# Second-stage products of a fused retention and MLP kernel cut in two, and the figures of its plan set anew

## The chip, the cores and the metric

The kernel runs on one core of a Trainium2 chip, in one launch. The metric is the device time of the launch in microseconds, the median of the runs. TensorE (PE in the profile) multiplies, VectorE (DVE) and ScalarE (ACT) work on what it leaves in PSUM, GpSimd (POOL) and SyncE (SP) issue the DMAs.

## The reference

The first part is retention, attention without a softmax: for each of 8 batches and 8 heads, over 576 positions and 64 dimensions. Its output, with the heads side by side, is the input of an MLP of 4608 tokens, 512 wide, with 2048 hidden units and the exact gelu.

```python
scores = scale * np.matmul(q, k.transpose(0, 1, 3, 2))
gamma = 1.0 - 2.0 ** (-5.0 - np.arange(H))
Dmat = np.where(rel >= 0, gamma[:, None, None] ** rel[None, :, :], 0.0)   # rel = i - j
x = np.matmul(scores * Dmat, v)              # to (4608, 512)
h = x @ w_in                                 # (4608, 2048)
g = 0.5 * h * (1.0 + erf(h / sqrt(2)))
out = g @ w_out                              # (4608, 512), float32
```

## The kernel before

**Work.** The 4608 tokens are nine blocks of 512 (t = 0 to 8), four units of 128 tokens each. For a unit, q and k are turned (by TensorE for the first ten units, by a transposing DMA after that), TensorE makes the scores (tile sc), VectorE multiplies them by the mask (ret), TensorE adds what lies within the chunk and what comes from the running state (o_ps, u_ps), and VectorE or ScalarE writes the result as a part of xT. The values scaled by the decay (vh) are made by ScalarE for the units in VH_ACT, in eight small instructions, and by VectorE for the others, in one.

**First MLP stage.** x times w_in. Blocks 0 and 1 take it plainly. From block 2 on the hidden units come in four parts, kp = 0 to 3, and each part is done in one of two ways. Either plainly, as 16 products of 512 columns with their gelus (`laid`, "p3" in LAYOUTS). Or as a set of seven products of half size in place of eight, by Strassen's scheme (`unit`, `add_chain`): 28 products of 256 columns on sums of x (xs) and of w_in (wi_sum), in three PSUM banks Y, Z and X. VectorE and ScalarE work between the products: the product 4 may only be added to its bank when q has been formed, 5 when the bank Y has been copied (m3), 6 when dif has been formed, 7 when the gelu c21 has read the bank Z (BEHIND). In LAYOUTS "0" is the set of part 0 by itself, "12" two sets woven, "p3" the plain part 3.

**Second MLP stage.** g times w_out, also by seven half-size products from block 1 on (FAST). The tokens of a block are cut into two halves, the columns of w_out as well; sums of g (tile s, `g_sum`) and of w_out (w_sum) are made by VectorE. A product p of SECOND = "1267534" contracts over four parts kp of two rows of 128, for each of r = 0 and 1: eight products of 256 columns. `fast` (line 1144) issues these eight in one piece. The sums of g stand in two tiles, one for kp 0 and 1 and one for kp 2 and 3, and a piece waits for both. VectorE and ScalarE bring the banks together (`add_second`), and SP stores the rows.

**What sets the order.** A planner in the kernel itself (class Plan, and the loop at the end) gives each step a duration, what it depends on and a due time, and runs engine by engine through time as it issues the instructions. What it reckons has no effect on the chip but through the order in which each engine's instructions stand. The figures: HOT is the time up to which TensorE is reckoned at half clock (`slow`), FETCH and BUSY_FETCH what the refill of a page of TensorE's instructions is reckoned to take (`paged`, PAGE = 127.8 products), 0.1 us for a change of array mode (`pe_time`, `run_woven`), GAP_A and GAP_B the least distance between two attention steps made of many small products, APART the groups whose scores are not woven with the step before, LOOK how many pieces ahead the loop may pick, HOLD, BEFORE, LEAD, SPREAD and EASE due times, SLACK how far a later step may be preferred by its due time. ORDER is the order of the loads on POOL's queue; of these, at most eight are on their way at once (`room_to_fly`). While the loads of the opening arrive, `warm` fills TensorE's gaps with products of zeros.

In a piece of the second stage:

```python
for kp in range(4):
    for kk in range(2):
        product(c[:, at, :], lhsT=left(t, p, kp)[:, kk, r * 128:r * 128 + 128],
                         rhs=right(p, kp)[:, kk, :], ...)
```

Of the kernel before, what the change touches and what calls it, by code (L numbers as in the profile page):

```python
# [107 lines left out]
def kernel(  # L108
# [23 lines left out]
    N_BLK = n_tok // TOK  # L132
# [28 lines left out]
    def slot_of(i):  # L161
# [3 lines left out]
    n = v_order.index(pair_of[1, 1][0])  # L165
# [5 lines left out]
    N_VH = 5  # L171
    N_RET = 3
    N_Q = 4
    VH_ACT = [5, 6, 7, 8, 9, 10, 16, 17, 19, 20, 23, 25, 27, 29, 30, 31, 32, 33, 34, 35, 36, 37]
    HOT = 9.2
    N_WARM = 8
    SLACK = 0.05
    CUTS = (0, 128, 256, 384, 512)
    AHEAD = 5
    VH_DUE = 14.0  # L180
    PARTS = 4
    FAST = 1
    FETCH = 3.5
    BUSY_FETCH = 6.2
    GAP_A = 1.6
    GAP_B = 1.6
    APART = [6, 7]
    BEFORE = 3.7
    UNIT_FROM = 2
    LOOK = 6  # L190
    HOLD = 5.0
    LAYOUTS = {2: ['0', '12', 'p3'], 3: ['0', '12', 'p3'], 4: ['01', '2', 'p3'], 5: ['01', '2', 'p3'], 6: ['23', '0', 'p1'], 7: ['0', '12', 'p3'], 8: ['0', '12', 'p3']}
    LEAD = 8
    SPREAD = 6.7
    EASE = 9
    ORDER = ("q1 q2 pos k2 q3 k3 v3 wi0 k1 wi4 v2 v1 wi5 wi1 wi2 wi3 wi6 v4 k5 wi7 q5 q4 wo0 k4 v5 wo4 wo1 wo5 wo2 "
             "q9 wo6 q6 wo7 v10 v7 q8 k7 v6 wo3 k6 v9 q7 k10 k9 v8 k8 q10").split()
    K_ORDER = [0, 1, 8, 9, 2, 3, 10, 11, 4, 5, 12, 13, 6, 7, 14, 15]
    PRODUCTS = "3251467"
    SECOND = "1267534"  # L200
    LAYOUT = {t: ["p0", "p1", "p2", "p3"] for t in range(2, N_BLK)}
    for t in range(UNIT_FROM, N_BLK):
# [15 lines left out]
    P = Plan()  # L218
    P.later = {}
    T = P.T  # L220
# [24 lines left out]
    banks = [f"b{n}" for n in range(8)]  # L245
# [57 lines left out]
    stream = []  # L303
    for t in range(N_BLK):
        if t < 2:
            cuts = CUTS if t == 0 else (0, 256, 512)
            for lo, hi in zip(cuts, cuts[1:]):
                stream.append([("1", t, m, 2, lo, hi) for m in K_ORDER[::2]])
        else:
            stream.append([one for block in LAYOUT[t] for one in laid(t, block)])  # L310
        if t < FAST:
            stream.append([("2", t, ts, m, m + 2) for m in range(0, N_DF, 2) for ts in range(2)])
            stream.append([("2", t, ts, m, m + 4) for ts in range(2, 4) for m in range(0, N_DF, 4)])
        else:
            stream.append([("2", t, p, r, n) for n, p in enumerate(SECOND) for r in range(2)])

    def piece_time(one):
        if one[0] == "u":
            return 4 * 0.1092
        if one[0] == "1":  # L320
            return one[3] * N_DM * ((one[5] - one[4]) / 2400 + 0.0025)
        return 8 * 0.1092 if isinstance(one[2], str) else (one[4] - one[3]) * 0.2158

    W0 = 14.0
    W = {}
# [27 lines left out]
    pos = const.tile([128, 1, NCI], FP32, name="pos")  # L353
# [518 lines left out]
    land = {}  # L872
# [268 lines left out]
    def rows_at_once(t):  # L1141
        return [(0, 1)] if t < N_BLK - 1 else [(0,), (1,)]

    def fast(one):
        _, t, p, r, _ = one
        rs = next(x for x in rows_at_once(t) if r in x)
        alone = p in "12"
        c = chain_of(("2", t, rs), [128, 1 if alone else len(rs), HALF], f"A{r}" if alone else BANK2[p])
        at = 0 if alone else r - rs[0]
        for kp in range(4):  # L1150
            for kk in range(2):
                product(c[:, at, :], lhsT=left(t, p, kp)[:, kk, r * 128:r * 128 + 128],
                                 rhs=right(p, kp)[:, kk, :], start=(p in OPENS and at + kp + kk == 0),
                                 stop=(kp == 3 and kk == 1), skip_group_check=True)
        if p == SECOND[-1] and r == 1:
            for two in range(2):
                g_ring[two].give(T["pe"] + 0.3)
                s_ring[two].give(T["pe"] + 0.3)
# [153 lines left out]
    for run in stream:  # L1312
        for one in run:
# [16 lines left out]
                    add_chain(("u", t, kp), 2, {q_: [f"mlp{('u', t, kp, q_)}"] for q_ in PRODUCTS},  # L1330
                              {q_: W["u", t, kp, q_] for q_ in PRODUCTS})
            elif isinstance(one[2], str):
                _, t, p, r, n = one
                rs = next(x for x in rows_at_once(t) if r in x)
                key = f"c{('2', t, rs)}"
                deps = []
                if p in G_SUM:
                    deps += [f"gs{t},{two}.{G_SUM[p]}" for two in range(2)]
                else:
                    deps += gelus_of(t, range(4), int(p != "1"))  # L1340
                deps += [f"ws{kp}.{W_SUM[p]}" for kp in range(4)] if p in W_SUM else []
                deps += [f"land wo{kp + 4 * (p != '1')}" for kp in range(4)] if p in "123" else []
                deps += [key + BEHIND2[p] + (str(r) if p == "2" else "")] if p in BEHIND2 else []
                add(nm, "pe", piece_time(one), deps, lambda one=one: fast(one), W[one], DRAIN,
                    banks=int(p == "1" or p in OPENS and r == rs[0]))
                if p == SECOND[-1] and r == rs[-1]:
                    at_ = {q_: {x: W["2", t, q_, x, SECOND.index(q_)] for x in rs} for q_ in SECOND}
                    add_second(("2", t, rs), len(rs), {q_: [f"mlp{('2', t, q_, x, SECOND.index(q_))}" for x in rs] for q_ in SECOND},
                               {q_: max(at_[q_].values()) for q_ in SECOND})
# [90 lines left out]
    in_macro = {nm for m in macros for nm in m[1]}  # L1440

    mode = ["full"]
    stretch_end = [0.0]

    def slow():
# [18 lines left out]
    def run_woven(names, start):  # L1464

        T["pe"] = start
        T["pe"] = T["now"] = start + weave(names) + (0.1 if mode[0] != "quad" else 0.0)
# [59 lines left out]
    def begun(one):  # L1527

        if one[0] == "u":
            return one[3] in "321" or BANK_OF[one[3]] in chain.get(one[:3], ())  # L1530
        if one[0] == "2" and isinstance(one[2], str):
            rs = next(x for x in rows_at_once(one[1]) if one[3] in x)
            return one[2] in "12" or (one[2] in OPENS and one[3] == rs[0]) or BANK2[one[2]] in chain.get(("2", one[1], rs), ())
        return True

# [43 lines left out]
    while True:  # L1579
# [72 lines left out]
```

## Time and profile before

| | us |
|---|---|
| median of 3 runs | 284.89 |
| lowest, highest | 284.52, 285.73 |
| the profiled execution | 285.15 |
| its span, first to last instruction | 283.2 |
| TensorE busy | 274.2 |
| VectorE busy | 224.5 |
| ScalarE busy | 182.7 |
| GpSimd busy | 110.3 |

The time of the profiled execution is longer than its span by what lies around the instructions. A row of the order in time gives the start, the time to the end of the last of the merged instructions, engine, line, operation, what is written from what, the shape, the count, and in brackets the idle time before with what ended it. Nearly all products carry line 229, a helper; they are told apart by the tiles: hT, yT, zT and xT_ belong to the first stage, oT to the second, sc, o_ps, u_ps and qk_ps to attention, warm to the fillers.

### The profile page before, as it was taken

To read this page: it belongs to the slowest core of one execution; us is meant where nothing else is said; L and a number is where in the kernel's file an instruction comes from. 1 tells how busy PE (TensorE), PEld (TensorE's weight loads), DVE (VectorE), ACT (ScalarE), POOL (GpSimd) and SP (SyncE) were. 2 spreads that over 40 slices of the span, in tenths; PEclk is the share of its full clock that TensorE was granted. 3 is DMA by queue.
4 is the path that set the end of the run, shared out by engine and by line. 5 is a ranking of instruction groups with operands and counts; after the bars stand their busy time and mean duration, and the time that the engine had idled before them with its cause. 6 is when DMAs were issued, how large, how long until landed. Compare 5 with 4: busy or idle time off the path is not lost.

```text
span 283.2 us, 8896 instructions
## 1 busy us (share of the span) xinstructions
PE 274.2 (97%) x3707; PEld 219.8 (78%) x3721; DVE 224.5 (79%) x430; ACT 182.7 (65%) x458; POOL 110.3 (39%) x139
## 2 busy tenths in 40 slices
PE   7999999999999999999999999999999999999993
PEld 2579848678888688868886888687868886888782
DVE  5760392689999997999799998986997788769832
ACT  7678805987318934795299329943898489727740
POOL 8966779809944059701426701905000000000000
PEclk9999999999999999999999999999999999999999
DMA  9999999999999999999999995999700040012013
GB/s 146 165 187 178 193 176 163 167 185 161 145 129 179 196 103 145 148 241 108 140 185 88 130 152 169 117 137 135 192 2 2 11 144 0 5 62 89 0 39 111
DMA packets 152071, 35.57 MB, mean 126 GB/s; under 512 B 141024, under 2 KB 147680, under 8 KB 152032
## 3 DMA queue, kind: packets, MB, share of 16 engines
q0 software_dynamic: 115792, 17.97, 96.2%
q1 hardware_dynamic: 35200, 16.78, 33.5%
q8 instruction: 29, 0.48, 0.8%
q10 hardware_dynamic: 1040, 0.26, 0.4%
q14 instruction: 10, 0.08, 0.1%
HBM read 36.70 MB, written 9.44 MB: 163 GB/s over the span
## 4 chain that ended last, share of the span: by engine, by line
PE 78%; DMA 11%; POOL 6%; issue 2%; ACT 1%; DVE 1%; POOLq 0%; ACTq 0%
PE oT L229 37%; PE hT L229 11%; PE zT L229 9%; DMA w_in<-in_moe_w_in_dram 6%; PE yT L229 6%; PE o_ps L229 4%; POOL qk_ld L517 3%; DMA w_out<-in_moe_w_out_dram 3%; PE sc L229 3%; PE u_ps L229 2%; DMA qk_ld<-in_k_dram 2%; POOL v_ld L517 1%; ACT g L1209 1%; PE qk_ps L233 1%; DVE t L568 0%
## 5 line engine op out<-in xcount | busy, mean ns | idle before, releaser
L229 PEld LDWEIGHTS <-w_in 128*128 128x128 bf16 x664 | 54.2, 98 | 14.8 <-issue 0.3
L229 PEld LDWEIGHTS <-g 128*128 128x128 bf16 x576 | 54.9, 98 | 12.5
L229 PE MATMUL hT<-xT,w_in 128*128 128x128 bf16 (+2 forms) x488 | 56.1, 267 | 0.4
L229 PEld LDWEIGHTS <-wi_sum 128*128 128x128 bf16 x420 | 40.9, 98 | 7.2 <-issue 0.9
L1099 ACT ACTIVATE g<-hT 128x512 bf16<-128x512 f32 (+1 forms) x76 | 37.9, 510 | 13.3 <-PE hT L229 11.5
L229 PE MATMUL oT<-w_out,g 128*128 128x256 bf16 (+1 forms) x315 | 44.0, 293 | 0.2 <-issue 0.2
L824 ACT ACTIVATE vh<-v_ld,dv 128x64 bf16<-128x64 bf16 x160 | 44.0, 344 | 0.0
L517 POOL DMA_DIRECT2D qk_ld<-in_q_dram x31 | 28.2, 909 | 39.7 <-DMA qkT<-qk_ld 29.9
L229 PEld LDWEIGHTS <-s 128*128 128x128 bf16 x384 | 36.9, 98 | 5.7 <-issue 1.0
L517 POOL DMA_DIRECT2D v_ld<-in_v_dram x31 | 28.3, 915 | 17.3 <-ACT vh L824 13.2
L229 PE MATMUL oT<-w_sum,s 128*128 128x256 bf16 x256 | 31.5, 273 | 0.7 <-issue 0.7
L1240 ACT COPY o_sb<-oT 128x512 f32<-128x512 f32 (+1 forms) x27 | 14.5, 539 | 26.9 <-PE oT L229 16.7
L229 PE MATMUL oT<-w_sum,g 128*128 128x256 bf16 x256 | 30.8, 273 | 0.0
L517 POOL DMA_DIRECT2D qk_ld<-in_k_dram x31 | 28.3, 914 | 1.5 <-DMA w_in<-in_moe_w_in_dram 0.6
L1209 ACT ACTIVATE g<-zT 128x512 bf16<-128x512 f32 x42 | 24.5, 619 | 0.4
L652 DVE TENSOR_TENSOR ret<-sc,msk 128x512 bf16<-128x512 f32 x36 | 23.0, 680 | 0.9 <-PE sc L229 0.9
L1244 DVE TENSOR_TENSOR o_sb<-o_sb,oT 128x512 f32<-128x512 f32 (+1 forms) x27 | 16.7, 623 | 8.3 <-PE oT L229 4.0
L570 ACT COPY q<-yT 128x512 f32<-128x512 f32 x17 | 9.9, 590 | 18.3 <-PE yT L229 18.3
L855 DVE TENSOR_TENSOR xT<-o_ps,dqT 128x512 bf16<-128x512 f32 x26 | 16.7, 680 | 3.0 <-PE o_ps L229 3.0
L568 DVE COPY qkT<-qk_ps 128x512 bf16<-128x512 bf16 x16 | 6.2, 418 | 15.4 <-PE qk_ps L233 15.4
L1218 DVE TENSOR_TENSOR zT<-q,zT 128x512 f32<-128x512 f32 x21 | 14.5, 692 | 1.6 <-PE zT L229 1.4
L829 ACT CAST u_sb<-u_ps 128x512 bf16<-128x512 f32 x15 | 8.8, 584 | 10.7 <-PE u_ps L229 7.1
(165 smaller groups left out, 457.7 us busy)
## 6 DMA issues: line engine op xcount, KB each, us to landing
out_dram<-o_sb SPq DMA_DIRECT2D x30, 256.0 KB, 4.1
qk_ld<-in_q_dram POOLq DMA_DIRECT2D x31, 128.0 KB, 6.5
qk_ld<-in_k_dram POOLq DMA_DIRECT2D x31, 128.0 KB, 6.3
v_ld<-in_v_dram POOLq DMA_DIRECT2D x31, 128.0 KB, 6.6
w_in<-in_moe_w_in_dram POOLq DMA_DIRECT2D x8, 256.0 KB, 8.3
w_out<-in_moe_w_out_dram POOLq DMA_DIRECT2D x8, 256.0 KB, 8.6
out_dram<-o_sb SPq DMA_DIRECT2D x12, 128.0 KB, 2.5
v_ld<-in_v_dram POOLq DMA_DIRECT2D x8, 64.0 KB, 5.7
```

The lines of the kernel that those rows point to most:

```text
L229: return nc.tensor.matmul(*args, **more)
L517: nc.gpsimd.dma_start(dst, src[2 * bp + j, :, ci * C:ci * C + C, :].rearrange("h s d -> s h d"))
L570: nc.scalar.copy(dst, src)
L652: nc.vector.tensor_tensor(r, t, by, op=ALU.mult)
L824: nc.scalar.activation(vh[:, h], loaded[i][1][:, h], AF.Copy, scale=dv[:, h, ci:ci + 1])
L829: ins = (nc.vector.tensor_copy if engine == "dve" else nc.scalar.copy)(u_sb[t if bp >= FINE else ci % 2], u_bank[1])
L855: nc.vector.tensor_tensor(dst, o, dqT[:, :, ci * C:ci * C + C], op=ALU.mult)
L1099: nc.scalar.activation(g_of(t, m0)[:, m0 % 2:m0 % 2 + n, m0 // 8, lo:hi], hT, AF.Gelu)
L1209: nc.scalar.activation(target(key, what), chain[key][n][1], AF.Gelu)
L1218: nc.vector.tensor_tensor(to, chain[key]["q"], z, op=ALU.add)
L1240: nc.scalar.copy(target(key, what), chain[key][n][1])
L1244: nc.vector.tensor_tensor(to, to, chain[key][n][1], op=ALU.add)
```

## The change

A piece of the second stage becomes two, part 0 for kp 0 and 1 and part 1 for kp 2 and 3. Each waits only for the sums of g, the gelus and the weights that it reads. The pieces of one product stay in their order. The figures of the plan, the parts of the first stage that are done as sets of seven (LAYOUTS: block 7 has four sets and no plain part), the units whose vh ScalarE makes, and the order of the loads are set anew; the change of mode is reckoned at 0.13 us (CHANGE), and loads that land early get 0.3 us of margin in the plan.

```diff
-    VH_ACT = [5, 6, 7, 8, 9, 10, 16, 17, 19, 20, 23, 25, 27, 29, 30, 31, 32, 33, 34, 35, 36, 37]
-    HOT = 9.2
+    VH_ACT = [5, 8, 12, 14, 15, 17, 19, 20, 26, 28, 30, 31, 32, 35, 37]
+    HOT = 10.1
-    SLACK = 0.05
+    SLACK = 0.3
-    FETCH = 3.5
+    FETCH = 4.0
-    GAP_A = 1.6
-    GAP_B = 1.6
-    APART = [6, 7]
-    BEFORE = 3.7
+    GAP_A = 4.2
+    GAP_B = 1.5
+    APART = [3, 6, 7]
+    BEFORE = 0.4
-    LOOK = 6
-    HOLD = 5.0
-    LAYOUTS = {2: ['0', '12', 'p3'], 3: ['0', '12', 'p3'], 4: ['01', '2', 'p3'], 5: ['01', '2', 'p3'], 6: ['23', '0', 'p1'], 7: ['0', '12', 'p3'], 8: ['0', '12', 'p3']}
+    LOOK = 16
+    HOLD = 4.6
+    LAYOUTS = {2: ['0', '12', 'p3'], 3: ['01', '2', 'p3'], 4: ['2', '30', 'p1'], 5: ['01', '2', 'p3'], 6: ['10', '2', 'p3'], 7: ['01', '23'], 8: ['3', '20', 'p1']}
-    SPREAD = 6.7
-    EASE = 9
-    ORDER = ("q1 q2 pos k2 q3 k3 v3 wi0 k1 wi4 v2 v1 wi5 wi1 wi2 wi3 wi6 v4 k5 wi7 q5 q4 wo0 k4 v5 wo4 wo1 wo5 wo2 "
-             "q9 wo6 q6 wo7 v10 v7 q8 k7 v6 wo3 k6 v9 q7 k10 k9 v8 k8 q10").split()
+    SPREAD = 7.1
+    EASE = 6.5
+    ORDER = ("q3 q2 k3 q1 pos v2 k2 wi0 k1 wi4 v3 v1 wi1 wi3 wi5 v4 wi2 wi6 k4 wi7 q4 wo0 q5 k5 v5 wo4 wo1 q9 q8 "
+             "wo5 v7 wo6 k7 wo7 v10 wo2 q6 v6 k6 wo3 q7 k10 q10 k8 k9 v9 v8").split()
-    PRODUCTS = "3251467"
+    PRODUCTS = "3251647"
...
-            stream.append([("2", t, p, r, n) for n, p in enumerate(SECOND) for r in range(2)])
+            stream.append([("2", t, p, r, n, part) for n, p in enumerate(SECOND) for r in range(2) for part in range(2)])
...
-        return 8 * 0.1092 if isinstance(one[2], str) else (one[4] - one[3]) * 0.2158
+        return 4 * 0.1092 if isinstance(one[2], str) else (one[4] - one[3]) * 0.2158
...
-        for kp in range(4):
+        for kp in (2 * part, 2 * part + 1):
...
-        if p == SECOND[-1] and r == 1:
+        second_left[t] -= 1
+        if not second_left[t]:
...
+                kps = (2 * part, 2 * part + 1)
                 if p in G_SUM:
-                    deps += [f"gs{t},{two}.{G_SUM[p]}" for two in range(2)]
+                    deps += [f"gs{t},{part}.{G_SUM[p]}"]
                 else:
-                    deps += gelus_of(t, range(4), int(p != "1"))
+                    deps += gelus_of(t, kps, int(p != "1"))
...
+    CHANGE = 0.13
...
-        return d + (0.1 if op.mode != mode[0] else 0.0)
+        return d + (CHANGE if op.mode != mode[0] else 0.0)
...
-            pad = MARGIN if op.name[0] == "v" and at > 40.0 else 0.0
+            pad = MARGIN if op.name[0] == "v" and at > 40.0 else 0.3 if flying[-1].end < 10.0 else 0.0
```

More of the change, by code (lines that the diff above doesn't have):

```diff
@@ L1142, in rows_at_once @@
         return [(0, 1)] if t < N_BLK - 1 else [(0,), (1,)]
+    second_left = dict.fromkeys(range(N_BLK), 28)
     def fast(one):
-        _, t, p, r, _ = one
+        _, t, p, r, _, part = one
         rs = next(x for x in rows_at_once(t) if r in x)
@@ L1332 @@
             elif isinstance(one[2], str):
-                _, t, p, r, n = one
+                _, t, p, r, n, part = one
+                kps = (2 * part, 2 * part + 1)
                 rs = next(x for x in rows_at_once(t) if r in x)
@@ L1337 @@
                 if p in G_SUM:
-                    deps += [f"gs{t},{two}.{G_SUM[p]}" for two in range(2)]
+                    deps += [f"gs{t},{part}.{G_SUM[p]}"]
                 else:
-                    deps += gelus_of(t, range(4), int(p != "1"))
-                deps += [f"ws{kp}.{W_SUM[p]}" for kp in range(4)] if p in W_SUM else []
-                deps += [f"land wo{kp + 4 * (p != '1')}" for kp in range(4)] if p in "123" else []
+                    deps += gelus_of(t, kps, int(p != "1"))
+                deps += [f"ws{kp}.{W_SUM[p]}" for kp in kps] if p in W_SUM else []
+                deps += [f"land wo{kp + 4 * (p != '1')}" for kp in kps] if p in "123" else []
                 deps += [key + BEHIND2[p] + (str(r) if p == "2" else "")] if p in BEHIND2 else []
                 add(nm, "pe", piece_time(one), deps, lambda one=one: fast(one), W[one], DRAIN,
[L1345 to L1348, printed above, removed]
+                    banks=int(not part and (p == "1" or p in OPENS and r == rs[0])))
+                if p == SECOND[-1] and r == rs[-1] and part:
+                    at_ = {q_: {x: W["2", t, q_, x, SECOND.index(q_), 1] for x in rs} for q_ in SECOND}
+                    add_second(("2", t, rs), len(rs), {q_: [f"mlp{('2', t, q_, x, SECOND.index(q_), 1)}" for x in rs] for q_ in SECOND},
                                {q_: max(at_[q_].values()) for q_ in SECOND})
@@ L1466, in run_woven @@
         T["pe"] = start
-        T["pe"] = T["now"] = start + weave(names) + (0.1 if mode[0] != "quad" else 0.0)
+        T["pe"] = T["now"] = start + weave(names) + (CHANGE if mode[0] != "quad" else 0.0)
         mode[0] = "quad"
@@ L1532, in begun @@
             rs = next(x for x in rows_at_once(one[1]) if one[3] in x)
+            if one[5]:
+                return P.ops[f"mlp{(*one[:5], 0)}"].end is not None
             return one[2] in "12" or (one[2] in OPENS and one[3] == rs[0]) or BANK2[one[2]] in chain.get(("2", one[1], rs), ())
```

## The prediction

> **What bounds the kernel now.** I read the page first, then who waited for whom on TensorE, then its order in time.
>
> ```profile
> span 283.2 us, 8896 instructions
> PE 274.2 (97%) x3707; PEld 219.8 (78%) x3721; DVE 224.5 (79%) x430; ACT 182.7 (65%) x458; POOL 110.3 (39%) x139
> ...
> PE 78%; DMA 11%; POOL 6%; issue 2%; ACT 1%; DVE 1%; POOLq 0%; ACTq 0%
> ```
>
> TensorE is busy 97% of the span and carries 78% of the chain that ended last. A "busy" PE may hide waits, so the second view is its waits after 60 us:
>
> ```profile
> PE oT L229 <- issue: 0.7, 1, 0.7
> PE zT L229 <- ACT g L1209: 0.4, 2, 0.2
> ```
>
> It names 1.1 us in 223. So the time is the number of products times their spacing, plus an opening that depends on loads, plus a tail. A change of order can win back only the few waits that are left; it can lose any amount. The spacing, from products that follow each other without a gap:
>
> ```profile
> 250.01 1.91 PE L229 MATMUL oT<-w_out,s 128*128 128x256 bf16 x16
> 251.76 1.91 PE L229 MATMUL oT<-w_sum,g 128*128 128x256 bf16 x16
> ...
> 263.59 2.75 PE L229 MATMUL hT<-xT,w_in 128*128 128x512 bf16 x12
> 266.18 3.66 PE L229 MATMUL oT<-w_out,g 128*128 128x256 bf16 x32
> ```
>
> Sixteen products of 256 columns take 251.76 - 250.01 = 1.75 us, so 0.109 each; twelve of 512 take 2.59, so 0.216 each. Starts are read, not durations, because a product's recorded length overlaps the next one.
>
> **The change part by part.** The built order of both programs is known; I counted in it.
>
> *Fewer products.* Block 7 computes its first stage with four sets of seven products ('01', '23') where it had three sets and a plain quarter. Out go 16 products of 512 columns (3.45 us), in come 28 of 256 (3.06): -0.39. The swap also puts four more steps on VectorE; its gelus take the place of others.
>
> At this swap a rule speaks against the change. The Trainium skill, page "TensorE: Matmul & The Clock Gate", section "Back-to-back issue gap", gives about 131 ns for a 512-column product in a sustained stream; by it the 16 would save only 2.10 us and the swap would cost about 0.96, an estimate that mixes the page's figure with the row's 0.109. The 0.216 above decides against that figure here, and for the same section's formula for a single gap.
>
> *Changes of array mode.* Products on quarters of the array stand between those on the whole array:
>
> ```profile
> 188.80 0.60 PE L229 MATMUL oT<-w_sum,s 128*128 128x256 bf16 x4
> 189.33 0.22 PE L229 MATMUL u_ps<-vh,qk_ld 64*64 64x64 bf16 x2
> ...
> 192.36 1.16 PE L229 MATMUL oT<-w_sum,s 128*128 128x256 bf16 x9
> 194.19 0.93 PE L229 MATMUL oT<-w_sum,s 128*128 128x256 bf16 x7 [0.68 <-issue]
> ```
>
> Four products from 188.80 end their turns at 189.24; the next starts at 189.33: 0.09 for one change. The order has 73 such changes from the first hT on, now 71: -0.19 at 0.095 each. CHANGE = 0.13 is thus more than the row shows, but it is only the plan's figure and costs no time by itself.
>
> *The wait for instructions.* From 192.36 nine products end at 193.34 and the tenth starts at 194.19: 0.85 lost, and no semaphore is named. The plan's page figure (a refill each 127.8 products) puts an edge there, after about 128 products of which most are short ones. The after has the same stretch with the same order, two long products more and two short ones fewer between the edges (about 0.2 us more cover). I take -0.2. Bounds: -0.85 if it goes, +0.85 if a second one like it appears. FETCH = 4.0 and GAP_A = 4.2 only tell the plan of it.
>
> *Waits inside the seven-product sets.* In a set, product 7 (zT from xs and wi_sum) needs the gelu of what product 4 (zT from xs and w_in) finished.
>
> ```profile
> 115.30 0.60 PE L229 MATMUL zT<-xs,w_in 128*128 128x256 bf16 x4
> 116.17 0.60 PE L229 MATMUL zT<-xT,wi_sum 128*128 128x256 bf16 x4
> 116.34 0.59 ACT L1209 ACTIVATE g<-zT 128x512 bf16<-128x512 f32 x1
> 116.98 0.60 PE L229 MATMUL zT<-xs,wi_sum 128*128 128x256 bf16 x4 [0.21 <-ACT g L1209]
> ...
> 228.95 0.60 PE L229 MATMUL zT<-xs,w_in 128*128 128x256 bf16 x4
> 230.26 0.60 PE L229 MATMUL yT<-xT,wi_sum 128*128 128x256 bf16 x4
> 230.40 0.62 ACT L1209 ACTIVATE g<-zT 128x512 bf16<-128x512 f32 x1
> 231.07 0.60 PE L229 MATMUL zT<-xs,wi_sum 128*128 128x256 bf16 x4 [0.21 <-ACT g L1209]
> ```
>
> Four products from 116.17 are through at 116.61, and 7 starts at 116.98: 0.37 lost; likewise 230.70 to 231.07: 0.37. Both stand in blocks that open with a single set (3 and 7). Blocks 4, 5 and 6 open with two sets woven together, and the view of the waits counts no third. The after opens blocks 3 and 7 with two sets: from the end of 4 to the start of 7 stand 1.31 and 2.18 us of products, as in blocks 4 to 6, not the 0.87 of block 3. The new '2','30' of block 4 has 1.75, as block 8 had, without a wait. So -0.74. One place gets worse: in the second pair of block 7 only 0.83 us stand between a 4 and its 7. In block 3 of the trace 7 came 1.24 us after the end of 4 (115.74 to 116.98), in block 7 1.68 after (229.39 to 231.07). So +0.4 to +0.85 if the gelu is queued as there, near 0 if ScalarE is free; I take +0.2, nearer to free, since the copies ahead of it there are spread over two engines.
>
> PRODUCTS with 6 ahead of 4 is a rank among ready pieces; what it moved is in these counts.
>
> *The split.* Each product of the second stage becomes two pieces of four, the first waiting for the first half of g and its sums alone. No product is added. In blocks 2, 5 and 7 four products of "6" move ahead of the last sixteen of "1" and "2"; in block 7 that takes the place of the plain quarter that had covered the last gelus. There the last 7 ends 3.3 us of products ahead of the first piece that reads its gelu, and 5.5 ahead of the first that reads its sums. Its VectorE step and gelu take about 0.7 + 0.6 by the rows of this part and of VectorE below, two sums 1.3 more. So 0, covered; without that cover each is late by what it lacks. A piece that waits holds every product behind it, since TensorE takes them in order. From the first product of block 8 to the end the order is the same product for product, so the tail costs 0.
>
> *The opening.*
>
> ```profile
> 11.12 1.48 PE L229 MATMUL warm<-u_sb 128*128 128x512 bf16 x3
> 12.39 0.57 PE L233 MATMUL qk_ps<-ident,qk_ld 128*128 128x128 bf16 x4
> 13.55 0.41 PE L229 MATMUL o_ps<-ret,v_ld 128*64 128x128 bf16 x8 [0.25 <-PE sc L229]
> ...
> 14.22 0.93 PE L229 MATMUL warm<-u_sb 128*128 128x512 bf16 x5
> 14.99 0.61 PE L229 MATMUL hT<-xT,w_in 128*128 128x128 bf16 x8
> ```
>
> Fillers still take 0.42 each at 11.12 (half clock; HOT = 9.2 told the plan otherwise). The after has three 512 fillers fewer and one of 128 more ahead of the first hT: 0.59 at full clock, 1.2 at half. But the first hT also needs a mask and a copy after o_ps. I take half, -0.3; bounds -1.0 and +0.5.
>
> *Loads and the moved attention steps.* POOL's queue is reordered; the attention steps of the first 60 us stand up to 4 us of products earlier, and two transposing DMAs on SP now stand before the first four stores.
>
> ```profile
> 37.61 0.88 POOL qk_ld L517
> ...
> 44.54 1.34 POOL qk_ld L513 x2
> ...
> qk_ld<-in_q_dram POOLq DMA_DIRECT2D x31, 128.0 KB, 6.5
> ...
> 47.16 0.76 DVE L568 COPY qkT<-qk_ps 128x512 bf16<-128x512 bf16 x2 [4.81 <-PE qk_ps L233]
> ```
>
> In the plan a load is issued when the one eight places before it has landed; between 37.61 and 44.54 seven were issued, about 1.0 us each, so a load lands 1.0 us sooner for each place gained. The tightest that I found is q8: issued at 37.61, landed 6.5 later at 44.1, its transposes through just before the copies at 47.16. In the after it stands 7 places earlier (landing 37.1) and its transposes 9.0 us of products earlier (about 37.9). So 0, covered by slack of about 0.8 us; a load that is late costs about 1 us. All other plan figures (SLACK, LOOK, HOLD, BEFORE, SPREAD, EASE, APART, VH_ACT) act through the order alone.
>
> **Sum.** -0.39 - 0.19 - 0.2 - 0.74 + 0.2 - 0.3 = -1.62. The profiled execution took 285.15 (span 283.2 and 1.95 around it), so 283.5; it lay 0.26 above the median 284.89, from which the sum gives **283.3**.
>
> **Rivals.**
>
> *VectorE becomes the bound* (slower). The multiplications "vh" on VectorE go from 16 to 22.
>
> ```profile
> core 0: us, PE busy (x) PEld busy (x) DVE busy (x) ACT busy (x) POOL busy (x), PEclk, DMA share, GB/s
> 14.00:60.00 46.00, 45.44 (x688) 34.88 (x691) 23.57 (x52) 31.88 (x90) 32.41 (x41) 1.00 1.90 177
> 60.00:84.40 24.40, 24.36 (x372) 20.58 (x371) 24.40 (x51) 11.80 (x27) 16.35 (x20) 1.00 2.04 153
> 226.90:253.60 26.70, 26.44 (x353) 21.56 (x352) 20.73 (x36) 19.04 (x49) 0.00 (x0) 1.00 0.11 34
> ...
> 265.24 0.69 DVE L999 TENSOR_TENSOR s<-s,g 128x1024 bf16<-128x1024 bf16 x1
> 265.85 0.69 DVE L999 TENSOR_TENSOR g<-g 128x1024 bf16<-128x1024 bf16 x1
> ```
>
> VectorE has no idle moment from 60 to 84.4, at whose end the sums for block 2 must be ready; one step takes 0.61 by the starts of the last two rows. From the point where VectorE is still full when block 2 is due, each step put in costs its full 0.6; six cost 3.6: 283.3 + 3.6 = **286.9**. For it: 24.40 of 24.40. Against: only three of the six, net, stand ahead of block 2, two of those right after the sums of w_out, and from 14 to 60 us VectorE is busy 23.57 of 46; in block 7 the added steps (two "vh", four of the fourth set) bring 20.7 to some 24 of 26.7 us. Chance 0.18.
>
> *A load comes late.* The slack of about 0.8 us is used up; one or two loads at 1.0 us, and nothing later to win them back: 284.3 to 285.3, **284.8**. Against: the trace shows no wait on a load after the opening. Chance 0.08.
>
> *The clock.* The opening is at half clock until 12.4 (0.42 a filler) and full at 14.22 (3 long and 2 short fillers in 0.77). With fewer fillers before it the full clock may come some 3 us later; the 2.6 us from 12.39 to 14.99 would take up to twice as long, half of it hidden by masks: +1.3, **284.6**. The Trainium skill, same page, section "Part 1: The HAM clock gate (the "warmup" mystery)", says that a free-running window of about 3.4 us with a busy array releases the clock; by it the moment also moves from run to run. Chance 0.07.
>
> *It does not do what it says.* The two waits of 0.37 come back at other sets, because the same engines serve the same chains and only the places moved: -1.62 + 0.74 + 0.4 leaves -0.5, **284.4**. Chance 0.07.
>
> **How the numbers follow.** The forecast, 283.3, has 0.60, with 282.0 to 284.4 as its own range. What a measurement of this kernel can tell from no change is about 0.5%, 1.42 us: below 283.47 is faster, above 286.31 slower. The forecast lies close to that bound: of its 0.60 I put 0.43 below and 0.17 above. A fetch wait that goes and an opening that gains its whole bound would give 281.9. So faster 0.43; same 0.17 + 0.08 + 0.07 + 0.07 = 0.39; slower 0.18. The range runs from 281.9 into the VectorE case, to 286.2, and leaves out some 0.2.
>
> **What would show it.** Right: in blocks 3 and 7 no wait of zT on a gelu above 0.2; 28 more products of 256 columns and 16 fewer of 512; first hT before 14.9; VectorE with idle time just ahead of block 2; the fetch wait still there, about 0.6. Wrong: a wait of TensorE on VectorE or on a load anywhere after 15 us, above all at the start of block 2 or at the transposes of q8; a second wait with no semaphore; in block 7 the second pair's 7 late by 0.4 or more.

## The result, and the profile after

| | before | after |
|---|---|---|
| median, us | 284.92 (6 runs) | 282.70 (6 runs) |
| lowest, highest | 283.96, 285.73 | 282.60, 282.95 |
| the profiled execution | 285.15 | 282.72 |
| its span | 283.2 | 280.7 |

The ratio is 0.9925, 95% interval 0.9905 to 0.9945: faster by 0.75%, 2.2 us. In the experiments below the kernel before ran again 29, 32 and 18 times, in three later series: medians 284.12, 284.23 and 284.21, single runs from 282.85 to 286.88. The forecast was 283.3.

Two things in this table are worth more than the ratio. The time fell by more than the forecast. And the spread fell from 1.8 us to 0.35. Both have to be explained.

The page of the changed kernel, its first lines and its chain of work:

```profile
span 280.7 us, 8896 instructions
PE 273.9 (98%) x3731; PEld 220.0 (78%) x3731; DVE 230.1 (82%) x438; ACT 174.0 (62%) x414; POOL 110.4 (39%) x139
...
PE 87%; DVE 4%; POOL 4%; DMA 3%; issue 1%; ACT 0%; POOLq 0%; DVEq 0%
```

TensorE's share of the chain went from 78% to 87%, DMA's from 11% to 3%. The long transfers on the chain of before lie in its first 50 us (w_in, w_out and a k), so most of what changed on the chain lies there. TensorE's waits after 15 us:

```profile
PE hT L229 <- DMA w_in<-in_moe_w_in_dram: 0.3, 1, 0.3
PE oT L229 <- ACT o_sb L1243: 0.2, 1, 0.2
```

Both rows of before (a wait with no releaser, 0.7, and two on gelus) are gone; two others have come, one on a load.

**Where the two traces part.** To compare them I set the two kernels beside each other at the first product of block 2's sets. The rows are of before, then of after:

```profile
84.78 0.38 PE L229 MATMUL yT<-xs,w_in 128*128 128x256 bf16 x2
```

```profile
83.04 0.27 PE L229 MATMUL yT<-xs,w_in 128*128 128x256 bf16 x1
```

The built order of after has four products of 256 columns more behind this place than before has, beside the exchange in block 7; they are worth 0.44. So after is 84.78 - 83.04 - 0.44 = 1.30 ahead when block 2 begins. From here to the start of the last product (278.30 and 275.81) it takes 275.81 - 83.04 - 0.44 = 192.33 against 193.52: 1.19 more. The forecast had 0.49 up to here (opening 0.3, changes of mode 0.19; both of the changes that went lie before block 2) and 1.13 after it.

**The opening**, of after:

```profile
11.31 0.88 PE L229 MATMUL warm<-u_sb 128*128 128x512 bf16 x4
12.03 0.39 PE L233 MATMUL qk_ps<-ident,qk_ld 128*128 128x128 bf16 x4
...
13.56 0.61 PE L229 MATMUL hT<-xT,w_in 128*128 128x128 bf16 x8
...
19.18 1.01 PE L229 MATMUL hT<-xT,w_in 128*128 128x128 bf16 x15 [0.26 <-DMA w_in<-in_moe_w_in_dram]
```

The fillers at 11.31 (three of 512 columns and one of 128) are through in 0.72, so at full clock; in the trace of before those at 11.12 still took 0.42 each. The first hT stands at 13.56 instead of 14.99. At 19.18 TensorE waits for a load of w_in: the last product before it starts at 18.71 and needs 0.056, so 0.42 is lost.

The clock can be read directly as well. Each trace keeps a record of the clock that was granted to TensorE. It begins with the full clock, at 12.77 us in before and 11.18 in after; for the time ahead of that it has no entry, and the profile's PEclk counts it as 1.00. The spacing of the products changes at the same moments.

**The sets.** In block 3 of after, product 7 comes without a wait:

```profile
115.29 1.04 PE L229 MATMUL zT<-xs,w_in 128*128 128x256 bf16 x8
116.17 0.60 PE L229 MATMUL yT<-xs,w_in 128*128 128x256 bf16 x4
116.60 0.60 PE L229 MATMUL zT<-xT,wi_sum 128*128 128x256 bf16 x4
117.04 0.60 PE L229 MATMUL zT<-xs,wi_sum 128*128 128x256 bf16 x4
```

Eight products take 0.88 from row to row and four 0.43 or 0.44, their own time: nothing is lost. Block 7 looks the same, its second pair too.

**The instruction wait.** Sixteen products that before had with a pause of 0.85 inside:

```profile
191.10 2.09 PE L229 MATMUL oT<-w_sum,s 128*128 128x256 bf16 x16
193.03 1.91 PE L229 MATMUL oT<-w_out,s 128*128 128x256 bf16 x16
```

They take 1.93 instead of 1.75: 0.18 is left of it.

**A new wait**, in block 4, TensorE and, ahead of it, VectorE:

```profile
160.10 0.39 PE L229 MATMUL o_ps<-qkT,u_sb 64*64 64x128 bf16 x16
160.70 0.60 PE L229 MATMUL oT<-w_sum,s 128*128 128x256 bf16 x4 [0.21 <-ACT o_sb L1243]
```

```profile
158.42 0.69 DVE L999 TENSOR_TENSOR s<-g,s 128x1024 bf16<-128x1024 bf16 x1
159.33 0.70 DVE L1238 TENSOR_TENSOR oT<-oT,q 128x512 f32<-128x512 f32 x1 [0.22 <-issue]
159.94 0.68 DVE L999 TENSOR_TENSOR s<-g,s 128x1024 bf16<-128x1024 bf16 x1
```

The product at 160.70 starts 0.60 after the row before it. In a trace without the wait (e9, below) that takes 0.32, so 0.28 is lost. The product waits for a copy on ScalarE, which waits for VectorE's step at 159.33; and that step starts 0.91 after the one before it, where VectorE's steps here follow each other in 0.60. "issue" says that no semaphore held it, and the semaphores that it waits for had indeed been raised by 158.89. So one VectorE instruction that is 0.31 late becomes 0.28 on TensorE. (Some expectations below call this wait 0.42; they counted the change of array mode ahead of the product as a loss.)

### The profile page after: what moved, and what is told of

It reads as the page before. It is cut to its first block, busy times and chain, and to the rows that moved or that the text cites. A ratio compares the mean times of both kernels' runs of the same rounds, so it can differ in the third digit from the quotient of the medians.

```text
span 280.7 us, 8896 instructions
## 1 busy us (share of the span) xinstructions
PE 273.9 (98%) x3731; PEld 220.0 (78%) x3731; DVE 230.1 (82%) x438; ACT 174.0 (62%) x414; POOL 110.4 (39%) x139
## 4 chain that ended last, share of the span: by engine, by line
PE 87%; DVE 4%; POOL 4%; DMA 3%; issue 1%; ACT 0%; POOLq 0%; DVEq 0%
PE oT L229 39%; PE hT L229 16%; PE zT L229 10%; PE yT L229 7%; PE o_ps L229 4%; DMA w_in<-in_moe_w_in_dram 3%; PE sc L229 2%; POOL qk_ld L517 2%; PE u_ps L229 2%; DVE s L999 1%; PE qk_ps L233 1%; DVE ret L652 1%; POOL v_ld L517 1%; POOL w_in L523 1%; DVE g L999 0%
## 5 line engine op out<-in xcount | busy, mean ns | idle before, releaser
L229 PEld LDWEIGHTS <-w_in 128*128 128x128 bf16 x656 | 53.0, 98 | 13.3 <-DMA w_in<-in_moe_w_in_dram 0.4
L229 PE MATMUL hT<-xT,w_in 128*128 128x128 bf16 (+2 forms) x480 | 53.5, 266 | 0.3 <-DMA w_in<-in_moe_w_in_dram 0.3
L229 PEld LDWEIGHTS <-wi_sum 128*128 128x128 bf16 x440 | 42.8, 98 | 6.6
L1099 ACT ACTIVATE g<-hT 128x512 bf16<-128x512 f32 (+1 forms) x72 | 35.9, 505 | 19.5 <-PE hT L229 17.7
L229 PE MATMUL oT<-w_out,g 128*128 128x256 bf16 (+1 forms) x320 | 45.6, 294 | 0.0
L229 PE MATMUL oT<-w_sum,s 128*128 128x256 bf16 x256 | 32.4, 273 | 0.2 <-ACT o_sb L1243 0.2
L824 ACT ACTIVATE vh<-v_ld,dv 128x64 bf16<-128x64 bf16 x112 | 31.2, 346 | 1.0 <-DMA v_ld<-in_v_dram 1.0
L1212 ACT ACTIVATE g<-zT 128x512 bf16<-128x512 f32 x44 | 25.9, 614 | 0.1
L821 DVE TENSOR_TENSOR vh<-v_ld,dv 128x512 bf16<-128x512 bf16 x22 | 15.0, 688 | 3.4 <-DMA v_ld<-in_v_dram 3.4
L1191 DVE TENSOR_TENSOR q<-q,zT 128x512 f32<-128x512 f32 x22 | 14.5, 684 | 1.7 <-PE zT L229 0.8
```

The costliest lines, as they stand in the source:

```text
L229: return nc.tensor.matmul(*args, **more)
L821: nc.vector.tensor_tensor(vh, loaded[i][1], dv[:, :, ci:ci + 1].to_broadcast([128, H, D]), op=ALU.mult)
L824: nc.scalar.activation(vh[:, h], loaded[i][1][:, h], AF.Copy, scale=dv[:, h, ci:ci + 1])
L1099: nc.scalar.activation(g_of(t, m0)[:, m0 % 2:m0 % 2 + n, m0 // 8, lo:hi], hT, AF.Gelu)
L1191: nc.vector.tensor_tensor(q_, q_, chain[key]["Z"][1], op=ALU.subtract)
L1212: nc.scalar.activation(target(key, what), chain[key][n][1], AF.Gelu)
```

## Experiments

Twelve kernels, in three series; each series ran on one chip with the kernel before beside it. The single runs of one kernel that carries the changed figures lie 0.2 to 1.1 apart; I read differences of medians under 0.2 as none.

**e1: the split alone**, in the kernel before, all figures as they were.

```diff
-        for kp in range(4):
+        for kp in (2 * part, 2 * part + 1):
...
-                    deps += [f"gs{t},{two}.{G_SUM[p]}" for two in range(2)]
+                    deps += [f"gs{t},{part}.{G_SUM[p]}"]
```

> The kernel before, with the split alone: each product of the second stage in two pieces, every figure as before. My theory, that the split carries nothing and the order carries all: 284.9, within 0.3 of the kernel before, since the program has the same 3721 products and the same 73 changes of array mode, and in the trace of before no product of the second stage waits on the sums of g. Rival, that the split carries the gain: about 282.7 to 283.5.

Measured: 283.56 (283.15 to 285.27), ratio 0.9995 (0.9976 to 1.0014). The medians lie 0.56 apart, the means, which the ratio goes by, 0.15: the split alone gives nothing that can be told from no change. Its one profiled execution took only 283.46, though, and its opening shows why. It has the same order as before's up to here:

```profile
9.89 0.60 PE L229 MATMUL warm<-u_sb 128*128 128x512 bf16 x3
10.33 0.39 PE L233 MATMUL qk_ps<-ident,qk_ld 128*128 128x128 bf16 x4
10.55 0.81 PE L229 MATMUL warm<-u_sb 128*128 128x512 bf16 x3
11.20 0.39 PE L233 MATMUL qk_ps<-ident,qk_ld 128*128 128x128 bf16 x4
...
13.61 0.61 PE L229 MATMUL hT<-xT,w_in 128*128 128x128 bf16 x8
```

The three fillers at 10.55 take 0.65, full clock, where before's three took 1.27. The clock rose 2.7 us sooner in this execution (10.10 by its record), and the first hT came 1.38 sooner, in an unchanged order. So the moment of the clock is not a property of the order, and my reading of one trace of before was a reading of a late one. From block 2 to the start of the last product, its trace takes 193.23 us, before's 193.52; the instruction wait, 0.50 here and 0.84 there, is that difference.

**e2: the changed kernel without the split**, all its figures kept (the diff of e1 the other way).

> The changed kernel with whole pieces, each behind both tiles of sums, all figures as in the changed kernel. The products are as many (264.6 us by their spacing in both) but the plan now places one set in block 4 and the last pair of block 7 with 0.87 between 4 and 7 instead of 1.75 and more. My theory: 283.1 to 283.5, that is 0.4 to 0.8 over the changed kernel, by waits of 0.37 on gelus at those sets and not by waits on the sums of g. Rival, that the split carries the gain: 284.5 or more, with waits of oT on the sums.

Measured: 284.19 (283.85 to 284.87), ratio 1.0006: the whole gain is gone, 1.6 over the changed kernel in e5. TensorE's waits after 20 us in its trace:

```profile
PE oT L229 <- ACT o_sb L1240: 0.4, 1, 0.4
PE oT L229 <- DVE ret L652: 0.3, 1, 0.3
PE oT L229 <- DVE s L999: 0.3, 1, 0.3
PE oT L229 <- issue: 0.3, 2, 0.2
PE zT L229 <- ACT g L1209: 0.2, 1, 0.2
```

(The row "issue" of two times 0.2, here and in e3 and e7, is no wait: at both places, near 52 and 57 us, the trace lacks the record of a product.) The set with 0.87 waits, as expected (0.38 at 143.5 us). But the larger part lies where pieces of the second stage wait: 0.56 at 76.4 for a copy, 0.40 at 161.9 put down to the mask step, 0.48 at 244.0 us for sums of g. My theory gave 283.1 to 283.5 and is wrong here; the rival is right as to the stage, though its 284.5 was not reached. Alone the split is worth nothing, under these figures it is worth most of the gain. Only the last of the three waits is one that the split itself would loosen. For the rest the plan, which builds another order with whole pieces, is the likely reason; no run separates the two.

**e3: the sets undone** in the changed kernel.

```diff
-    LAYOUTS = {..., 3: ['01', '2', 'p3'], 4: ['2', '30', 'p1'], ..., 6: ['10', '2', 'p3'], 7: ['01', '23'], 8: ['3', '20', 'p1']}
+    LAYOUTS = {..., 3: ['0', '12', 'p3'], 4: ['01', '2', 'p3'], ..., 6: ['23', '0', 'p1'], 7: ['0', '12', 'p3'], 8: ['0', '12', 'p3']}
-    PRODUCTS = "3251647"
+    PRODUCTS = "3251467"
```

> The changed kernel with the sets of the kernel before (LAYOUTS and PRODUCTS; block 7 has its plain part again, blocks 3 and 6 open otherwise). By the spacing +0.40. My theory: the wait of zT on a gelu in block 3 comes back (0.37), so 283.5, up to 283.9 if the woven pair of block 6, now with 0.87 between 4 and 7, waits as well. Rival, that the sets are worth the products alone: 283.1. Second rival, that the fourth set of block 7 costs as much on VectorE as it saves: 282.7.

Measured: 284.93 (284.6 to 285.7), 2.2 over the changed kernel, and more than any of the theories gave. After 20 us:

```profile
PE oT L229 <- ACT q L1230: 0.8, 1, 0.8
PE zT L229 <- ACT g L1212: 0.5, 2, 0.3
PE oT L229 <- issue: 0.3, 2, 0.2
PE yT L229 <- ACT q L570: 0.2, 1, 0.2
```

The wait in block 3 is back (0.37 at 115.7 us), but the largest row is a copy on ScalarE that ends late for the second stage at 214.1 us, and the last row stands at 170.4 us in block 5, whose sets are the same in both. Other sets put other work on ScalarE and VectorE, and what comes after them is placed elsewhere.

**e4: the loads and fillers undone** in the changed kernel: ORDER and HOT = 9.2 of the kernel before.

> The changed kernel with ORDER and HOT of the kernel before: the loads come as before and three more fillers of 512 stand in the opening (0.43 by the spacing at full clock). My theory, from the traces (the first product of block 2's attention, a 34 us mark, came 1.2 us earlier in the changed kernel): 283.9, the fillers back at half clock to 12.4 us and first hT near 15. Rival, that only the fillers count at full clock: 283.1. Second rival, that the opening is hidden later by loads: 282.7.

Measured: 282.49 (282.04 to 282.58), no worse than the changed kernel. Its fillers had come back (16 of 512 columns ahead of the first hT, as in before) and cost nothing in the end; the second rival is right. My theory, which gave the opening's 1.2 us to ORDER and HOT, is wrong.

**e5: the changed kernel again**, to see its spread.

> The changed kernel, unchanged. Since the same opening became full-clock at 12.4 us in the trace of before and at 10.1 us in that of the split alone, my theory is now that the moment of the clock is free in both kernels, that the kernel before pays for it (offset 8.1 against 6.7 us at its first hT, and runs from 283.0 to 285.1), and that the changed kernel hides it behind a load of w_in at 19.2 us: 282.7, all runs within 0.8. Rival, that the changed kernel is as exposed and its first six runs were early by chance: single runs spread over 1.5 to 2 us, median 283.2 or more.

Measured: 282.58 (282.01 to 282.85, 8 runs), ratio 0.9937 (0.9914 to 0.9961), beside 32 runs of before from 283.28 to 286.88. (An "offset", in that text, is a product's start less the sum of the spacings ahead of it.) All fourteen runs of the changed kernel lie within 0.95. What the moment of the clock does in the two openings, from the traces of all kernels that share them (the start of the full clock in the trace's record, the first hT, and the first product sc after 32 us):

| opening | trace | full clock from | first hT | sc |
|---|---|---|---|---|
| before's | before | 12.77 | 14.99 | 33.90 |
| | e12 | 11.75 | 14.42 | 33.33 |
| | e1 | 10.10 | 13.61 | 32.52 |
| the changed one | e7 | 12.11 | 14.06 | 32.74 |
| | after | 11.18 | 13.56 | 32.67 |
| | e2 | 10.44 | 13.40 | 32.79 |
| | e5 | 9.95 | 13.63 | 33.05 |
| | e9 | 9.77 | 13.37 | 32.05 |
| | e8 | 8.64 | 13.52 | 32.72 |
| | e10 | 7.92 | 13.52 | 33.03 |
| | e3 | 7.90 | 13.35 | 32.75 |

In before's opening 2.7 us of clock are 1.38 us at the column sc. In the changed one the column sc does not follow the clock: e3 and e7, 4.2 us of clock apart, reach it together. What comes early mostly waits for loads instead: after, e2, e3 and e8 wait for w_in near 19 us (0.42 to 0.70), e5 and e10 near 25.8 (0.73 and 0.82), and e7, the latest, at neither place. Only e9 is early and waits for no load after its first hT either; it is 0.6 ahead of all the others at sc. The view in order of time of e3, whose clock was the earliest:

```profile
8.31 0.40 PE L233 MATMUL qk_ps<-ident,qk_ld 128*128 128x128 bf16 x4
8.54 0.22 PE L229 MATMUL warm<-u_sb 128*128 128x128 bf16 x1
9.22 0.40 PE L233 MATMUL qk_ps<-ident,qk_ld 128*128 128x128 bf16 x4 [0.46 <-DMA qk_ld<-in_k_dram]
...
10.12 0.40 PE L233 MATMUL qk_ps<-ident,qk_ld 128*128 128x128 bf16 x4 [0.28 <-DMA qk_ld<-in_q_dram]
```

**e6: fewer fillers** in the kernel before.

```diff
-    HOT = 9.2
+    HOT = 10.1
```

> The kernel before with HOT = 10.1 alone: three fillers of 512 fewer and two of 128 more ahead of the first hT (0.54 less by the spacing at full clock), ORDER and sets as before. Theory that the fillers stood on the path: 0.5 to 1.1 faster than the kernel before, 283.0 to 283.6, with the spread between runs as wide as before or wider, since its loads are not later. Rival, that the opening waits for loads and masks anyway: 284.1, no change.

Measured: 284.54 (283.63 to 285.73), ratio 1.0000 (0.9978 to 1.0023). No gain: the rival's number. Its later order changed as well, so it says only that fewer fillers are not a gain by themselves.

**e7: six more vh on VectorE** in the changed kernel.

```diff
-    VH_ACT = [5, 8, 12, 14, 15, 17, 19, 20, 26, 28, 30, 31, 32, 35, 37]
+    VH_ACT = [5, 8, 12, 15, 19, 26, 30, 32, 37]
```

> The changed kernel with 28 of the multiplications vh on VectorE instead of 22 (six units taken out of VH_ACT). Same products; one place in block 3 goes to 0.87 between 4 and 7. Rival of the prediction, that VectorE is at the bound already: 0.6 for each of the six, 3.6, so 286.3. My theory, that VectorE has room again before block 2 and in block 7: 282.7 to 283.4.

Measured: 284.36 (283.86 to 284.63), 1.8 over the changed kernel: between the two, 0.3 for each step. After 20 us:

```profile
PE oT L229 <- ACT g L1212: 0.7, 1, 0.7
PE oT L229 <- DVE ret L652: 0.4, 1, 0.4
PE oT L229 <- issue: 0.3, 2, 0.2
```

TensorE now waits on VectorE at 102.2 us, and behind a gelu at 240.3 us. So the changed kernel has room on VectorE for its 22, and not for 28 in the order that the plan makes of them; where between the two the room ends was not tried.

**e8: block 7 with three sets and a plain part** in the changed kernel; nothing ahead of block 7 moves.

```diff
-    7: ['01', '23']
+    7: ['01', '2', 'p3']
```

> The changed kernel with block 7 as '01', '2' and its plain part 3: 16 products of 512 back in, 28 of 256 out, nothing moved ahead of block 7. The prediction's term: 0.39 slower, 283.1. Rival, that the 28 products of the fourth set lose as much again on VectorE and ScalarE: 282.7 or less. Second rival, that the plain part leaves the second stage of block 7 waiting on its sums: 283.5 or more.

Measured: 282.81 (282.35 to 283.03, 11 runs), 0.23 over e5 in the same series. The sign of the forecast's term, some 0.6 of its size; 0.23 is close to what can be told apart here.

**e9: block 3 opened by a single set**, nothing else, in the changed kernel.

```diff
-    3: ['01', '2', 'p3']
+    3: ['0', '12', 'p3']
```

> The changed kernel with block 3 opened by a single set again ('0', '12', 'p3' as before); nothing else moves and the products are as many. The prediction's term: the wait of zT on a gelu comes back at about 116 us, 0.37, so 0.37 over the changed kernel's 282.6: 283.0. Rival, that a wait of TensorE in the middle is won back at a later wait on VectorE (block 4 waits 0.4 at 160.7 us in any case): 282.6.

Measured: 282.35 (282.0 to 282.64, 7 runs): no loss. Its trace has the wait back and has lost the other one:

```profile
114.45 0.60 PE L229 MATMUL zT<-xT,wi_sum 128*128 128x256 bf16 x4
115.27 0.60 PE L229 MATMUL zT<-xs,wi_sum 128*128 128x256 bf16 x4 [0.21 <-ACT g L1212]
...
160.07 0.39 PE L229 MATMUL o_ps<-qkT,u_sb 64*64 64x128 bf16 x16
160.39 0.61 PE L229 MATMUL oT<-w_sum,s 128*128 128x256 bf16 x4
```

and VectorE, just before that:

```profile
158.40 0.68 DVE L999 TENSOR_TENSOR s<-g,s 128x1024 bf16<-128x1024 bf16 x1
159.00 0.69 DVE L1238 TENSOR_TENSOR oT<-oT,q 128x512 f32<-128x512 f32 x1
159.60 0.68 DVE L999 TENSOR_TENSOR s<-g,s 128x1024 bf16<-128x1024 bf16 x1
```

0.38 came back in block 3 and 0.28 went in block 4; the 0.1 that is left is less than can be told apart. From block 2 to the start of the last product the trace takes 192.67 us, after's 192.77. VectorE's step follows in 0.60 here. The rival's number, by a mechanism that it did not name: not a backlog worked off, but a VectorE instruction that is late by itself in one order and not in the other. The order of e9 has two more VectorE instructions than the changed kernel's, added in block 3. Its row from 150 to 162 us; the columns are the stretch, its length, then busy time and count of PE, PEld, DVE, ACT and POOL:

```profile
150.00:162.00 12.00, 12.00 (x231) 9.63 (x230) 12.00 (x22) 5.43 (x12) 10.43 (x12) 1.00 1.77 114
```

VectorE is busy all of the time here, and the step is not late. (e4 has 12.00 of 12 as well, and no wait.) So VectorE's load is not what made it late.

**e10: one unit's vh moved to ScalarE** in the changed kernel (unit 24 into VH_ACT), against that wait.

> The changed kernel with one unit's vh (unit 24) moved from VectorE to ScalarE, which is idle from 157.5 to 160 us in its trace; the same products in nearly the same order. Theory that VectorE is the bound from 150 to 162 us (busy 11.78 of 12 there) and makes the 0.42 wait of oT at 160.7 us: the wait goes or halves, 282.2 to 282.4. Rival, that the copy on ScalarE itself is late, or that VectorE refills with other work: 282.6, the wait still there.

Measured: 282.54 (282.32 to 282.75), the wait as long as it was. But the run does not test the theory: by the traces the step that left VectorE stood near 167 us, after the wait, and from 150 to 162 us VectorE is as busy as before (11.78). It is e9 and e4, above, that speak against the load. The pause of the same step stands in five traces with the wait (after, e5, e8, e10, e11) and in neither of two without it (e4, e9).

**e11: two fillers of 512 columns and one of 128 more** in the changed kernel (HOT = 9.2 alone).

> The changed kernel with HOT = 9.2 as before: two fillers of 512 and one of 128 more in the opening (0.49 by the spacing), the same products in the same sets after that. Theory that the opening of the changed kernel ends with the load of w_in at 19.2 us and not with its products or the clock: 282.6 to 282.8, the wait on w_in shorter by as much. Rival, that fillers stand on the path: 283.1 or more, with single runs spread wider.

Measured: 282.44 (282.34 to 282.53). The added 0.49 costs nothing. But the wait for w_in is not shorter, as the theory had it (0.44, for 0.42 in after); the clock of this execution rose at 8.69, 2.5 us sooner than in after, so the two traces don't show where the 0.49 was given up:

```profile
19.02 0.56 PE L229 MATMUL hT<-xT,w_in 128*128 128x128 bf16 x7 [0.28 <-DMA w_in<-in_moe_w_in_dram]
```

**e12: the sets alone**, in the kernel before (the diff of e3 the other way).

> The kernel before with LAYOUTS and PRODUCTS of the changed kernel, all else as before (whole pieces, its own figures). By the products 0.39 faster, and block 3 opens with two sets (0.37 faster); against that block 4 now has a set with 0.87 between 4 and 7, and block 7 a woven pair with 0.87. Theory that sets, figures and split only pay together: 283.6 to 284.3, within 0.6 of the kernel before (284.2). Rival, that the sets alone carry the gain, since undoing them cost 2.3: 282.6 or less.

Measured: 284.38 (283.1 to 286.5), ratio 1.0002 (0.9979 to 1.0026). No gain. In its trace the instruction wait is there, and the second stage of block 7 waits on a copy:

```profile
191.82 1.16 PE L229 MATMUL oT<-w_sum,s 128*128 128x256 bf16 x9
193.38 0.81 PE L229 MATMUL oT<-w_sum,s 128*128 128x256 bf16 x6 [0.41 <-issue]
...
240.06 1.36 PE L229 MATMUL oT<-w_out,g 128*128 128x256 bf16 x11
241.83 0.93 PE L229 MATMUL oT<-w_out,g 128*128 128x256 bf16 x7 [0.40 <-ACT q L1227]
```

## Why the prediction was right, and where it was not

The sign and nearly the size were right. Several of the terms were not, and their errors had both signs.

**Fewer products, -0.39.** Right in kind; e8 puts 0.23 on it.

**Changes of mode, -0.19.** Counted, not measured by itself.

**The instruction wait, -0.2: mis-sized.** With before's order there it is 0.84 (before), 0.50 (e1), 0.57 (e12) and nothing in e6 and e3, which have other numbers of products ahead of it. In the changed kernel it is 0.18 in one execution and nothing in the other (e5), and in e4 and e7 to e11 the same products lose at most 0.05. So it was worth about 0.5, not 0.2; I had put it only as far down as the added cover of 0.2. The sign that I had named for being right, a wait of about 0.6 that stays, did not show.

**The waits in the sets, -0.74: right in place, wrong in worth.** Both went, by 0.38 and 0.37, and the second pair of block 7 brought no new one (the term of +0.2 was nothing). But 0.28 came back in block 4, and e9 shows that block 3's part of the gain was worth nothing to the end that could be measured. The step that failed: I looked for the next late product inside the sets alone, and took a gap of the second stage that had not waited before (in block 4, 1.7 us from the end of product 6 to the start of 5, in both kernels) as safe.

**The split, 0: right for the split by itself (e1), wrong as a part of this change.** I counted what it moved in the built order and found the moves covered. What I didn't ask is what that order would have been without it. e2 does: 1.6 worse, with waits in the second stage at three places, one of them on sums. The same holds for the sets: undone they cost 2.2 (e3), added alone they give nothing (e12). Terms that were taken one at a time from the built order are costs of that order; they are not what each edit is worth.

**The opening, -0.3: mis-sized, and for a reason that one trace cannot show.** The two traces differ by 1.30 up to block 2. But e1 reached its first product of a set at 83.41 in before's own order, 1.37 sooner than before's trace. The mean of three traces with before's order up to there is 84.14 (before 84.78, e1 83.41, e12 84.22); that of eight with the changed one (after, e3, e5, e7 to e11) is 83.08, or 83.52 with the 0.44: 0.6, mode changes included. Neither ORDER nor HOT nor the fillers make it: e4, with those of before, reaches the place at 83.17 without the four products, e6 has no gain, e11 no loss. What did change is what the opening waits for: in the changed kernel an early clock mostly runs into loads, between 9 and 12 us (e3, e8, e10) and at 19 or 25.8, and is given up there, while in before's all of the opening moves with TensorE's clock. That would also make its runs lie closer together; with one trace of each kernel this is not shown. Which of the other figures does this is open: no run took SLACK, BEFORE, LOOK or the margin of 0.3 by itself, and e4, with before's loads and without the wait for w_in, is as narrow as the changed kernel.

On the clock, the Trainium skill, page "TensorE: Matmul & The Clock Gate", section "Part 1: The HAM clock gate (the "warmup" mystery)", says that the full clock comes about 4 us into sustained work, give or take 0.5 from run to run, after one busy window of about 3.4. The window shows in the records: the full clock lasts 269.65 us in twelve of the fourteen traces and 273.07 in the other two, 79 and 80 times 3.413. The free phase agrees with e1 against before. The size does not: the fillers run from 1.2 to 6.3 us in all these traces, with 0.06 between them. If that counts as busy, an estimate by the page's window puts the change at 8.0 at the latest (1.2 and two windows). The table has it from 7.9 to 12.8, more than one window apart, so a free phase alone does not explain it.

**VectorE as the bound** didn't come about, with 22 vh. But the sign that I named for it was a bad one. The rows of after, columns as above:

```profile
60.00:84.40 24.40, 24.40 (x376) 20.74 (x374) 24.40 (x54) 12.08 (x28) 15.42 (x19) 1.00 2.15 152
150.00:162.00 12.00, 11.79 (x228) 9.38 (x227) 11.78 (x21) 5.46 (x12) 10.44 (x12) 1.00 1.85 105
```

VectorE has no idle time ahead of block 2 here either, and TensorE doesn't wait for it. A full engine is not yet a late one. e7 shows how near it was: six steps more, 1.8.

**A late load.** The one wait on a load after 15 us (0.42 at 19.18) was in the list of what would prove me wrong. It didn't: e7, whose clock rose 0.9 later, has no such wait and reaches the column sc 0.07 later. The wait only takes back what the earlier clock had given. The wait at 160.70, behind a step of VectorE, was in that list too, and there the list was right: it is the 0.28 that the sum lacks.

**The tail, 0**: right; the last product starts 4.9 us before the end of the span in both.

**The sum.** Up to block 2: forecast -0.49, -1.30 between the two traces, -0.6 in the mean. After it: forecast -1.13, measured -1.19 between the two traces, and -0.90 against e1. The sum of -1.62 falls short of the medians' 2.2 and nearly meets the later series' 1.65. That is in part luck, since both hold an opening that was forecast too small and, after it, a set wait's worth too many and an instruction wait's too few, which cancel in part. The forecast of 283.3 was nearer than its terms.

## What to carry to other kernels

A kernel whose order comes from a planner has no parts that add up: the worth of an edit is found by undoing it in the new kernel, and by making it alone in the old one, and the two need not agree. Before a trace is used as the base of a sum, ask whether its opening is typical; a second trace of the same order stood 1.4 us apart here. And a wait that goes is a gain only if the next place that can be late, on another engine and in another stage, is counted as well.

## What was not expected of the hardware

An engine can be late with no semaphore in sight, and not TensorE alone. On TensorE it was 0.84, 0.50, 0.57 and nothing at one place of one order, and 0.18 or nothing in the changed one. There the traces speak for the supply of instructions. A DMA queue of its own moves them in pieces of 16 KB, 29 in a run. In the four traces with a pause such a piece lands at 192.76 (before), 191.28 (e1), 191.96 (e12) and 191.22 us (after), and the product behind the pause starts 1.43, 1.25, 1.42 and 1.36 later. In e6 the same product starts 1.31 after its piece, without a pause. So TensorE seems to go on some 1.3 us after the piece is there, and a late piece makes the pause: it took 1.60 us to arrive in before and 1.08 in after. No run changed this by itself.

On VectorE one step came 0.31 late in five traces (0.91 after the last, for 0.60) and on time in two whose order had changed ahead of it. In none of the five does a piece of instructions land in the 3 us ahead of it, so the cause there stays open.

The moment of the full clock moved from 12.77 to 10.10 us between two executions of one opening, and from 7.90 to 12.11 in another. Where the opening waits for TensorE, as before's does, half of that goes into the time.
